# Cosformer attention with a multiplicative FFN: the query features of one batch transposed by DMA instead of TensorE, and the next loads issued later

## The chip, the cores and the metric

The kernel runs on one core of a Trainium2 chip. The metric is the device time of one execution in microseconds (us), as the median of several runs; lower is better. The profiled execution has a span (first to last recorded instruction) that is a little shorter than its device time.

## The reference

There are 8 batches of 8 heads, 576 positions and 64 dimensions per head, in float32. Attention is linear: the features of a row are its rectified values times a cosine and times a sine of its position, side by side, so 128 features per head.

```
q_p = phi(q, cos_w, sin_w)              # max(q, 0) * cos | max(q, 0) * sin
k_p = phi(k, cos_w, sin_w)
kv  = einsum('bhsf,bhsd->bhfd', k_p, v)
z   = sum(k_p, axis=2)
num = einsum('bhsf,bhfd->bhsd', q_p, kv)
den = einsum('bhsf,bhf->bhs', q_p, z)[..., None] + 1e-06
attn = num / den                        # then heads side by side: x, 4608 x 512
a = x @ w1;  b = x @ w2                 # 512 x 1024 each
out = (a * b @ w3) @ w_out              # 1024 x 1024, 1024 x 512
```

## The kernel before, in words

**The feed-forward part.** The 4608 tokens are taken in nine tiles of 512 (`t` from 0 to 8). The kernel forms `w3 @ w_out` once (`w34b`), so a tile needs `a` and `b` for eight column blocks (line 438), their product `abT` (a ScalarE copy on line 475, a VectorE product on line 479), and four blocks of 128 tokens times `w34b` (line 484), which ScalarE copies to `osb` (line 490) and a DMA that GpSimd issues stores (line 423).

**The attention part.** A batch has five chunks of rows, four of 128 and one of 64. Its steps are: `load` (lines 112 and 114: k, q and v of a batch, two DMAs each, issued by GpSimd, converted to bf16 on the way); `prep_k` and `prep_q` (features of a chunk: the cosine half on VectorE, line 251, the sine half on ScalarE, line 255); `prep_v` (a copy, from batch 2 on by GpSimd, line 275); `kv_chunk` (line 283: kv and z, summed over the five chunks, copied to `kvs` on lines 288 and 289); the transpose of each q chunk, 8 heads of 128 features, into `qpT`; `num` (line 341: `qpT` times `kvs`, then VectorE normalises to `xblk`, lines 349 to 351); and `x_tr`, which transposes `xblk` into its place in the 512-token tile `xT` of the feed-forward part. From batch 2 on `x_tr` is a DMA transpose that SyncE issues (line 373).

**Two ways to transpose a q chunk.** `q_tr` does it by eight TensorE transposes into a PSUM tile `pst` (line 314), which VectorE copies to `qpT` (line 316). The other way is a DMA transpose that SyncE issues at the end of `prep_q` (line 269). `dma_q(b)` names the chunks of batch `b` that take the second way: none of batches 0 to 2, two of batch 3, three each of batches 4 to 6, all five of batch 7.

**The order.** It is written out by hand: every engine runs its instructions in the order in which the program issues them. The generator `ffn_groups(t)` issues tile `t` in 24 groups: 16 for `a` and `b` (even groups a block of `a`, odd ones a block of `b`), then 8 for the output blocks. After group `g` the list `slots[g]` is issued. `attention_at` puts the steps of a batch into these slots (`kv`, `tr`, `nu`, `xt` give the slot of each chunk), and `spread` deals feature steps evenly over a stretch of slots. While tile 1 is computed (`t == 1`), batch 2 goes through attention (q features and v copies in slots 0 to 4, `kv` in slots 2 to 6, `q_tr` in slots 3, 5, 7, 9 and 11, `num` and `x_tr` in slots 8, 10, 12, 14 and 17), the features of batch 3 are made in slots 6 to 23, and batch 4 is loaded. A slot says where an instruction stands in its engine's order, not when it runs: GpSimd and SyncE take theirs as soon as the data and buffers that they need are there.

`ld` has two buffers for each of k, q and v, so the load of batch 4 writes the buffers of batch 2 and waits until its features are made. `num` has one PSUM buffer of two banks (`ps_att`), so a `num` waits for the normalisation of the one before it. Tile 2 of the feed-forward part begins with the first three chunks of batch 2 as its last 384 tokens.

Of the kernel before, what the change touches and what calls it, by code (L numbers as in the profile page):

```python
# [68 lines left out]
def kernel(  # L69
# [12 lines left out]
    B = q.shape[0]  # L82
# [64 lines left out]
    def feature_buffers(i):  # L147

        va = const.tile([P, NCH, H, D + 2], BF16, name=f"va{i}")
        nc.vector.memset(va[:, :, :, D:D + 1], 1.0)  # L150
        nc.vector.memset(va[64:128, 4, :, 0:D], 0.0)
        va_bufs.append(va)
        for name, bufs in (("kp", kp_bufs), ("qp", qp_bufs)):
            fp = const.tile([P, NCH, H, F], BF16, name=f"{name}{i}")
            nc.vector.memset(fp[64:128, 4, :, :], 0.0)
            bufs.append(fp)
# [46 lines left out]
    def w3_tr(jp):  # L203
        pst = ps_tr.tile([P, 8, 128], BF16, name="pst")
        for lc in range(8):
            nc.tensor.transpose(pst[:, lc, :], w3b[:, jp, ts(lc, 128)], identb[:])
        w3T = wst.tile([P, 8, 128], BF16, name="w3T")
        nc.vector.tensor_copy(out=w3T[:], in_=pst[:])
        w3Ts[jp] = w3T
# [14 lines left out]
    def order_of(b):  # L224

        return [0, 1, 2, 3, 4] if b % 2 == 0 else [4, 0, 1, 2, 3]

    def dma_q(b):

        return order_of(b)[5 if b < 3 else 3 if b == 3 else 2 if b < B - 1 else 0:]  # L230

    feat = {}

# [31 lines left out]
    def prep_q(b, c):  # L265
        features(b, feat_of(b)[1], raw[b, "q"], c)
        if c in dma_q(b):
            R = ROWS[c]
            nc.sync.dma_start_transpose(out=att_of(b)["qpT"][:, :, ds(columns_of(b, c), R)],
                                        in_=feat[b][1][:R, c].rearrange("p h f -> p (h f)"))  # L270
# [38 lines left out]
    def q_tr(b, c, evac=True):  # L309
        R = ROWS[c]  # L310
        qp = feat[b][1]
        pst = ps_tr.tile([P, 8, 128], BF16, name="pst")
        for h in range(H):
            nc.tensor.transpose(pst[:, h, :], qp[:, c, h, :], identb[:])  # L314
        dst, src = att_of(b)["qpT"][:, :, ds(columns_of(b, c), R)], pst[:, :, 0:R]
        on_vector = lambda: nc.vector.tensor_copy(out=dst, in_=src)  # L316
        on_scalar = lambda: nc.scalar.copy(out=dst, in_=src)
        if evac:
            on_vector()
        return on_vector, on_scalar  # L320
# [10 lines left out]
    def num(b, c, chain=True):  # L331
        rows = out_rows(b, c)
        R = ROWS[c]
        at = columns_of(b, c) - rows.start
        qpT, kvs = att[b]["qpT"], att[b]["kvs"]
        if b == 0 and c == 0:
            nt = ps_first.tile([P, 2, 512], FP32, name="pfirst")
        else:
            nt = ps_att.tile([P, 2, 512], FP32, name="pnum")
        for h in range(H):  # L340
            nc.tensor.matmul(nt[:, h // 4, ds((h % 4) * 65, 65)], lhsT=qpT[:, h, ds(at, 128)],  # L341
                             rhs=kvs[:, h, :], start=True, stop=True)
        n4 = nt[rows, :, 0:260].rearrange("p g (h e) -> p g h e", e=65)
        xblk = sm.tile([P, 2, 4, D], BF16, name="xblk", bufs=4)
        att[b]["x"][c] = xblk

        def normalize():
            den = sm.tile([P, 2, 4], FP32, name="den")
            nc.vector.tensor_scalar_add(out=den[rows], in0=n4[:, :, :, 64], scalar1=1e-6)
            nc.vector.reciprocal(out=den[rows], in_=den[rows])  # L350
            nc.vector.tensor_tensor(out=xblk[rows], in0=n4[:, :, :, 0:D],  # L351
                                    in1=den[rows].unsqueeze(3).to_broadcast([R, 2, 4, D]),
                                    op=ALU.mult)

        if chain:
            normalize()
        return normalize
# [3 lines left out]
    def x_tr(b, c, by_vector=False):  # L361
        R, rows = ROWS[c], out_rows(b, c)
        xblk = att[b]["x"].pop(c)
        xf = xblk[rows].rearrange("p g h d -> p (g h d)")
        if b % 2 == 0:
            slot = S * b + 128 * c
        else:
            slot = S * b + (0 if c == 4 else 64 + 128 * c)
        t, o = divmod(slot, 512)
        if t not in xT:  # L370
            xT[t] = xtp.tile([P, 4, 512], BF16, name="xT")
        if b >= 2:
            nc.sync.dma_start_transpose(out=xT[t][:, :, ds(o, R)], in_=xf)
            return
        pst = ps_tr.tile([P, 8, 128], BF16, name="pst")
        for kc in range(4):
            nc.tensor.transpose(pst[:, kc, 0:R], xf[:, ts(kc, 128)], identb[rows, rows])
        copy = nc.vector.tensor_copy if by_vector else nc.scalar.copy
        copy(out=xT[t][:, :, ds(o, R)], in_=pst[:, 0:4, 0:R])  # L379
# [131 lines left out]
    def spread(units, first, last, slots):  # L511
        for i, u in enumerate(units):
            slots[min(last, first + int(i * (last + 1 - first) / len(units)))].append(u)
# [32 lines left out]
    for t in range(NT):  # L546
        slots = [[] for _ in range(24)]
        if t == 0:
            slots[1].append(lambda: x_tr(0, 1, by_vector=True))
            slots[1].append(lambda: q_tr(0, 3, evac=False)[1]())  # L550
            slots[1].append(lambda: num(0, 2))
            slots[3].append(lambda: x_tr(0, 2))
            slots[3].append(lambda: num(0, 3))
            slots[4].append(lambda: x_tr(0, 3))
            slots[6].append(lambda: prep_q(0, 4))
            slots[11].append(lambda: feature_buffers(1))
            slots[8].append(lambda: q_tr(0, 4))
            slots[10].append(lambda: num(0, 4))
            slots[12].append(lambda: x_tr(0, 4))
            slots[14].append(lambda: w3_tr(0))  # L560
            between = [[] for _ in range(32)]
            later = [[] for _ in range(24)]
            spread(prep_units(1, (prep_k,)), 6, 8, between)
            spread(prep_units(1, (prep_q,)), 10, 12, between)
            spread(prep_units(1, (prep_v,)), 13, 13, between)
            attention_at(1, between, kv=(14, 14, 14, 14, 15), tr=(12, 13, 17, 18, 19),
                         nu=(16, 17, 18, 20, 22), xt=(18, 19, 20, 22, 25))
            later[:8] = between[24:32]
            for jp in range(8):
                for part in range(2):  # L570
                    if part == 0 and jp < 7:
                        slots[15].append(lambda jp=jp: w3_tr(jp + 1))
                    slots[15].append(lambda jp=jp, part=part: w34_mm(jp, part))
                    slots[15] += between[2 * jp + part]
            for g in range(16, 24):
                slots[g] += between[g]
            slots[16].append(lambda: load(3, "kqv"))
            spread(prep_units(2, (prep_k,)), 20, 23, slots)
        elif t == 1:
            for g in range(24):  # L580
                slots[g] += later[g]
            spread(prep_units(2, (prep_q,)), 0, 4, slots)
            spread(prep_units(2, (prep_v,)), 0, 4, slots)
            attention_at(2, slots, kv=(2, 3, 4, 5, 6), tr=(3, 5, 7, 9, 11),
                         nu=(8, 10, 12, 14, 17), xt=(8, 10, 12, 14, 17))
            for g, name in ((1, "k"), (8, "q"), (15, "v")):
                slots[g].append(lambda name=name: load(4, name))
            each = [u for c in zip(*(prep_units(3)[i:i + NCH] for i in (0, 5, 10))) for u in c]
            spread(each, 6, 23, slots)
        else:  # L590
            if t + 3 < B:
                for g, name in ((1, "k"), (8, "q"), (15, "v")):
                    slots[g].append(lambda name=name: load(t + 3, name))
            if t + 1 < B:
                attention_at(t + 1, slots, kv=(0, 1, 2, 3, 4), tr=(2, 4, 7, 10, 13),
                             nu=(6, 8, 11, 14, 17), xt=(6, 8, 11, 14, 17))
            if t + 2 < B:
                each = [u for c in zip(*(prep_units(t + 2)[i:i + NCH] for i in (0, 5, 10))) for u in c]
                spread(each, 0, 22, slots)
        for g, _ in enumerate(ffn_groups(t)):  # L600
            for u in slots[g]:
                u()
# [30 lines left out]
```

## Time and profile before

| what | value |
|---|---|
| median of 9 runs | 258.79 us (258.68 to 259.16) |
| the profiled execution | 258.73 us, span 257.0 us |
| granted TensorE clock, mean | 0.996 |
| TensorE matmul busy | 247.0 us, 96% of the span |
| VectorE, ScalarE, GpSimd busy | 145.9, 128.0, 86.0 us |
| bytes moved by DMA | 37.11 MB |

PE is TensorE's matmul work, PEld its weight loads (which run beside it), DVE is VectorE, ACT is ScalarE, POOL is GpSimd, SP is SyncE; POOLq and SPq are the instruction queues that issue DMAs. A row of a timeline gives start and length in us, the engine, the line, and output and inputs by name. In a table by stretch the columns are the stretch, its length, and the busy time of each engine with the number of its instructions, then the granted clock, the busy share of the DMA engines and their rate. The share of a DMA queue can exceed 100%, since one engine has several packets under way.

### The profile page before, as it was taken

Reading aid. Unit: us, or ns where it says so; the run is one execution under the profiler, and the core shown is the slowest. Engines: PE = TensorE matmul, PEld = TensorE weight load, DVE = VectorE, ACT = ScalarE, POOL = GpSimd, SP = SyncE. Lnnn points to the kernel's source line nnn. Section 1 sums busy time; section 2 is a strip of 40 time slices with the busy share of each in tenths; the row PEclk is TensorE's granted clock in tenths of the full one; section 3 lists DMA queues with packets and bytes.
Section 4 is the critical chain, followed back from the end, with each engine's and each line's share of the span. In section 5 each row is a group of like instructions: output and inputs, shape, how many; then the busy total and the mean of one; then the engine's idle time right before and its main releaser. Section 6 shows DMA issues by size and latency. Waiting matters only on the chain.

```text
span 257.0 us, 5053 instructions
## 1 busy us (share of the span) xinstructions
PE 247.0 (96%) x1934; PEld 135.0 (53%) x1967; DVE 145.9 (57%) x346; ACT 128.0 (50%) x219; POOL 86.0 (33%) x147
## 2 busy tenths in 40 slices
PE   8889999999999999999999999999999999999992
PEld 2478565655565465546554645555455544444441
DVE  6875755757879549824871787278526614303310
ACT  2775326727956555555655465646523233323321
POOL 7665244530760583048205900700230031022000
PEclk9999999999999999999999999999999999999998
DMA  7999999999999599999998999826490252024025
GB/s 194 183 193 202 209 204 202 199 199 198 245 164 137 99 203 188 161 165 162 188 154 182 178 195 133 180 46 134 93 193 13 57 125 66 0 43 123 1 44 122
DMA packets 68025, 37.11 MB, mean 144 GB/s; under 512 B 35616, under 2 KB 64544, under 8 KB 68000
## 3 DMA queue, kind: packets, MB, share of 16 engines
q0 software_dynamic: 35488, 27.20, 65.9%
q1 hardware_dynamic: 32352, 9.44, 21.0%
q8 instruction: 15, 0.25, 0.4%
q10 hardware_dynamic: 160, 0.13, 0.2%
q14 instruction: 10, 0.08, 0.1%
HBM read 38.80 MB, written 9.44 MB: 188 GB/s over the span
## 4 chain that ended last, share of the span: by engine, by line
PE 72%; DMA 20%; issue 2%; ACT 2%; POOL 1%; DVE 1%; ACTq 0%; POOLq 0%
PE ffnps L438 42%; PE ffnps L484 21%; DMA ks<-in_k_dram 10%; DMA qs<-in_q_dram 7%; DMA w2b<-in_moe_w_dram 3%; PE pnum L341 3%; PE pnum L283 3%; PE pst L314 2%; ACT kp L255 1%; POOL vs L120 0%; PE ffnps L501 0%; ACT osb L503 0%; POOL w2b L190 0%; POOL w1b L178 0%; DVE xblk L351 0%
## 5 line engine op out<-in xcount | busy, mean ns | idle before, releaser
L479 DVE TENSOR_TENSOR abT<-asb,ffnps 128x512 bf16<-128x512 bf16 x68 | 46.4, 683 | 64.1 <-PE ffnps L438 57.6
L438 PE MATMUL ffnps<-xT,w1b 128*128 128x512 bf16 (+2 forms) x312 | 74.4, 357 | 0.9 <-DVE xT L379 0.3
L438 PE MATMUL ffnps<-xT,w2b 128*128 128x512 bf16 (+2 forms) x306 | 73.2, 357 | 0.5
L475 ACT CAST asb<-ffnps 128x512 bf16<-128x512 f32 x68 | 39.8, 585 | 63.1 <-PE ffnps L438 55.7
L484 PE MATMUL ffnps<-w34b,abT 128*128 128x512 bf16 x273 | 63.3, 379 | 0.4
L423 POOL DMA_DIRECT2D out_dram<-osb x42 | 22.3, 536 | 119.7 <-ACT osb L490 119.6
L438 PEld LDWEIGHTS <-w1b 128*128 128x128 bf16 x320 | 28.8, 98 | 27.5 <-issue 0.8
L484 PEld LDWEIGHTS <-abT 128*128 128x128 bf16 x280 | 26.5, 98 | 30.3 <-DVE abT L479 0.4
L438 PEld LDWEIGHTS <-w2b 128*128 128x128 bf16 x320 | 27.4, 97 | 22.7
L490 ACT COPY osb<-ffnps 128x512 f32<-128x512 f32 x35 | 20.5, 585 | 37.9 <-PE ffnps L484 36.7
L255 ACT ACTIVATE qp<-qs,sinv 128x512 bf16<-128x512 bf16 (+2 forms) x40 | 28.2, 716 | 1.5 <-DMA qs<-in_q_dram 1.5
L351 DVE TENSOR_TENSOR xblk<-pnum,den 128x512 bf16<-128x512 f32 (+1 forms) x39 | 26.9, 691 | 1.4
L255 ACT ACTIVATE kp<-ks,sinv 128x512 bf16<-128x512 bf16 (+1 forms) x35 | 24.9, 721 | 0.0
L341 PEld LDWEIGHTS <-qpT 128*128 128x128 bf16 x320 | 15.1, 98 | 8.9 <-DVE xblk L351 0.9
L275 POOL COPY va<-vs 128x512 bf16<-128x512 bf16 (+1 forms) x30 | 18.4, 642 | 0.0
L251 DVE TENSOR_SCALAR qp<-qs,cosv 128x512 bf16<-128x512 bf16 (+1 forms) x40 | 18.0, 456 | 0.6 <-DMA qs<-in_q_dram 0.6
L341 PE MATMUL pnum<-kvs,qpT 128*128 128x65 bf16 x312 | 16.5, 194 | 0.3 <-DVE kvs L289 0.3
L283 PEld LDWEIGHTS <-kp 128*128 128x128 bf16 x280 | 12.7, 98 | 5.2
L316 DVE COPY qpT<-pst 128x1024 bf16<-128x1024 bf16 (+1 forms) x20 | 12.4, 618 | 5.0 <-PE pst L314 4.9
L218 PE MATMUL ffnps<-woutb,w3T 128*128 128x512 bf16 x61 | 15.0, 379 | 0.1
L314 PEld LDWEIGHTS <-qp 128*128 128x128 bf16 x184 | 12.0, 98 | 4.7
L283 PE MATMUL pnum<-va,kp 128*128 128x65 bf16 x280 | 14.1, 194 | 0.0
(81 smaller groups left out, 179.2 us busy)
## 6 DMA issues: line engine op xcount, KB each, us to landing
out_dram<-osb POOLq DMA_DIRECT2D x16, 256.0 KB, 3.9
out_dram<-osb POOLq DMA_DIRECT2D x24, 128.0 KB, 3.0
qs<-in_q_dram POOLq DMA_DIRECT2D x9, 256.0 KB, 7.7
ks<-in_k_dram POOLq DMA_DIRECT2D x7, 320.0 KB, 6.3
qs<-in_q_dram POOLq DMA_DIRECT2D x7, 320.0 KB, 7.0
vs<-in_v_dram POOLq DMA_DIRECT2D x7, 320.0 KB, 8.6
w3b<-in_moe_w_dram POOLq DMA_DIRECT2D x8, 256.0 KB, 13.1
ks<-in_k_dram POOLq DMA_DIRECT2D x7, 256.0 KB, 7.2
```

Of the source, the lines that this page charges most:

```text
L251: nc.vector.tensor_scalar(out=dst[:R, c, :, 0:D], in0=src[:R, :, c, :], scalar1=0.0, scalar2=cosv[:R, at:at + 1], op0=ALU.max, op1=ALU.mult)
L255: nc.scalar.activation(out=dst[:R, c, 0:n, D:F], in_=src[:R, 0:n, c, :], func=ACTF.Relu, scale=sinv[:R, at:at + 1], bias=0.0)
L275: eng.tensor_copy(out=feat_of(b)[2][:R, c, :, 0:D], in_=raw[b, "v"][:R, :, c, :])
L283: nc.tensor.matmul(kvt[:, h // 4, ds((h % 4) * 65, 65)], lhsT=kp[:, c, h, :], rhs=va[:, c, h, 0:D + 1], start=(i == 0 and h % 4 == 0), sto ...
L341: nc.tensor.matmul(nt[:, h // 4, ds((h % 4) * 65, 65)], lhsT=qpT[:, h, ds(at, 128)], rhs=kvs[:, h, :], start=True, stop=True)
L351: nc.vector.tensor_tensor(out=xblk[rows], in0=n4[:, :, :, 0:D], in1=den[rows].unsqueeze(3).to_broadcast([R, 2, 4, D]), op=ALU.mult)
L423: on.dma_start(out=rows[:, :, cols], in_=osb[64 * i:64 * i + rows.shape[0], :, cols])
L438: nc.tensor.matmul(out, lhsT=w[:, kc, ts(jc, 128)], rhs=x[:, kc, tok], start=(kc == 0), stop=(kc == 3))
L475: nc.scalar.copy(out=asb[:], in_=aT[:, :])
L479: nc.vector.tensor_mul(out=abT[:, jc, :], in0=asb[:], in1=bT[:, :])
L484: nc.tensor.matmul(ops[:, :], lhsT=abT[:, jc, ts(ms, 128)], rhs=w34b[:, jc, :], start=(jc == 0), stop=(jc == 7))
L490: nc.scalar.copy(out=osb[:, ms % 2, :], in_=ops[:, :])
```

## The change

For batch 2 all five chunks of q are now transposed by DMA: `prep_q` issues the transpose on SyncE behind the features of each chunk (slots 0 to 4 of `t == 1`), and `attention_at` no longer issues `q_tr` for them. The loads of batch 4 go from slots 1, 8 and 15 to slots 8, 13 and 18.

```
-        return order_of(b)[5 if b < 3 else 3 if b == 3 else 2 if b < B - 1 else 0:]
+        return order_of(b)[5 if b < 2 else 0 if b == 2 else 3 if b == 3 else 2 if b < B - 1 else 0:]
...
-            for g, name in ((1, "k"), (8, "q"), (15, "v")):
+            for g, name in ((8, "k"), (13, "q"), (18, "v")):
                 slots[g].append(lambda name=name: load(4, name))
```

## The prediction

> **What bounds the kernel now.** I read the page first. TensorE is busy for 96% of the span, but so are the DMA engines until two thirds of it, so the two rows by slices don't settle which of them counts while batch 2 is worked on.
>
> ```profile
> PE 247.0 (96%) x1934; PEld 135.0 (53%) x1967; DVE 145.9 (57%) x346; ACT 128.0 (50%) x219; POOL 86.0 (33%) x147
> ...
> PE   8889999999999999999999999999999999999992
> ...
> DMA  7999999999999599999998999826490252024025
> ```
>
> Then the chain that ended last: up to 61.2 us it runs through DMAs, from 64.1 us to 251 us through TensorE almost without a break (the piece at 192.8 us, 0.67 us on ScalarE, is the exception). The change acts from 66 us on. So the question is what TensorE does in tile 1. I cut the trace at the first product of tiles 1, 2, 3 and of tiles 6, 7 (timeline of TensorE), and asked for the table by stretch.
>
> ```profile
> 64.13:90.14 26.01, 25.80 (x216) 14.24 (x220) 19.91 (x48) 17.88 (x31) 12.60 (x21) 1.00 0.98 162
> 90.14:114.76 24.62, 24.41 (x197) 13.28 (x200) 16.27 (x37) 13.58 (x23) 10.22 (x17) 1.00 1.11 180
> 187.27:210.55 23.28, 23.07 (x173) 11.94 (x176) 10.74 (x24) 7.30 (x13) 3.15 (x7) 1.00 0.39 83
> ```
>
> The reader should see that matmul time fills each of the three tiles (25.80 of 26.01 us in the first) at a full granted clock, and that they differ in length. Tile 1 holds five q transposes on TensorE, tile 2 three, tile 6 none: 24.62 - 23.28 = 1.34 us for three is 0.447 us a chunk. The timeline of TensorE shows the same from start to start: eight transposes take 76.30 - 75.86 = 0.44 us. (The 0.61 us beside them is the length up to the modelled end of the last, not the time they hold the engine.)
>
> ```profile
> 75.86 0.61 PE L314 MATMUL pst<-identb,qp 128*128 128x128 bf16 x8
> 76.30 1.03 PE L438 MATMUL ffnps<-xT,w1b 128*128 128x512 bf16 x4
> 77.17 0.42 PE L341 MATMUL pnum<-kvs,qpT 128*128 128x65 bf16 x8
> ```
>
> **What is removed.** Five chunks, 40 transposes: 5 x 0.447 = 2.23 us of TensorE in a stage where nothing else ends last. Five copies on VectorE (line 316, 3.1 us in all) go too. VectorE is the nearest other engine there: 9.72 of the 10 us from 74 to 84 are busy. In that window it loses 0.60 + 0.60 + 0.34 = 1.5 us (start to start), TensorE two transposes, 0.9 us; so 8.2 us of VectorE stand in 9.1 us and it doesn't become the bound on the mean. I count nothing for its relief, though two `num` in the window waited for `xblk` (0.9 us of weight-load idle, 0.1 us of matmul idle).
>
> **What is added: five DMA transposes.** A chunk is 256 KB (the last 128 KB). Their issue costs SP about 1.25 us each; SP has nothing before 76.98 us, where the first `xT` transpose stands, so no one queues behind them. ScalarE ends the sine halves of the five chunks at 66.9, 68.0, 69.1, 69.7 and 71.0 us, VectorE its cosine halves no later than 0.2 us behind. With 1.25 us each on SP the issues fall at about 66.9, 68.2, 69.4, 70.7 and 71.9 us. How long they take beside loads is the disputed cost, and these are the nearest rows:
>
> ```profile
> DMA to landing us min/median/max: 2.7/3.7/6.1
> ...
> q1 hardware_dynamic: 1413, 0.35, 70.6%
> q0 software_dynamic: 732, 0.38, 69.1%
> ```
>
> The first is line 269 over the 16 chunks of the other batches; the two others are the queues from 103 to 107 us, where loads (q0) and transposes (q1) run together and each moves about 0.09 MB a us. With the longest landing, 6.1 us, they are there at 73.0, 74.3, 75.5, 76.8 and 78.0 us. They are due where `num` starts, which today is 74.73, 77.17, 79.60, 81.73 and 84.70 us, less 0.447 us for each transpose gone ahead of it (3, 4, 5, 5, 5): 73.4, 75.4, 77.4, 79.5 and 82.5 us. So all five are in time, the first by 0.4 us, the third by 1.9 us. Low bound of the cost: nothing. High bound: no row shows five in a row beside loads, and a half-size `xT` transpose issued at 124.58 us, with loads under way, took 7.3 us; that case is the slow rival below. I take nothing, because the rows are nearer: in time order from 68.6 us, at 1.25 us a chunk and 1.73 MB of loads at the 198 GB/s of the load-only stretch from 40 to 60 us, the queue would be c0, c1, half of k (1.6 us), c2, the rest of k (1.3 us), c3, half of q (1.6 us), c4, and c2 ends at 74.0, c3 at 76.5, c4 at 78.8 us.
>
> The page "VectorE: DVE Perf Modes" of the Trainium skill, section "Rules for kernel authors", speaks against the change: it advises TensorE for a 128x128 transpose if a PSUM destination will do, and its section "The three transpose paths" gives 390 ns there and 1309 ns by DMA. By those figures, taken serially, a chunk of eight would need 10.5 us by DMA, the third would land near 100 us and the change would lose some 20 us; the trace differs, since no chunk took over 6.1 us from issue to landing.
>
> **The `xT` transposes** of batch 2 stand behind them on SP and in the ring. The one that matters is the third, the last that tile 2 needs: its `xblk` is ready at 81.7 - 2.2 = 79.4 us, and even with 7.3 us it is there at 86.7 us, where tile 2 begins at 90.14 - 2.23 = 87.9 us. It goes at nothing, with 1.2 us in hand.
>
> **The loads of batch 4.** GpSimd's timeline shows what slots mean for them.
>
> ```profile
> 66.01 1.17 POOL L275 COPY va<-vs 128x512 bf16<-128x512 bf16 x2
> 67.13 0.70 POOL L112 DMA_DIRECT2D ks<-in_k_dram  x1
> 67.82 0.71 POOL L114 DMA_DIRECT2D ks<-in_k_dram  x1
> 68.50 1.81 POOL L275 COPY va<-vs 128x512 bf16<-128x512 bf16 x3
> 71.32 0.68 POOL L112 DMA_DIRECT2D qs<-in_q_dram  x1 [1.01 <-ACT qp L255]
> ...
> 73.77 0.70 POOL L112 DMA_DIRECT2D vs<-in_v_dram  x1
> ```
>
> GpSimd runs ahead of TensorE: v, in slot 15, is issued at 73.8 us, when TensorE is only about to begin group 8. In the new order k stands behind all five copies of batch 2, so it goes out at about 68.9 us, 1.7 us later. q then follows two copies of batch 3 and still waits for the last q features of batch 2 (71.0 us): 71.4 us, as today. v follows at about 73.5 us. All three stay ahead of the store that waits until 85.78 us (slot 18 is the last before it), which would have been the trap. The gain from moving them is nothing, except 1.7 us of DMA time left to the first two transposes. The copies that move ahead of k come 1.4 us earlier and were not waited for. The loads will land later since they share with the transposes, by up to the 1.18 MB of the chunks, 6 us at 198 GB/s: today they land by 81.5 us, then by 87.5 us at worst; batch 4's features begin with tile 2, k first, and k is there near 76 us. Cost nothing, 6 us of cover for k and q.
>
> **The sum.** 258.73 (profiled run; span 257.0 and 1.7 around it) - 2.23 = 256.50; the median of the runs lies 0.06 above that execution, so 256.5 to 256.6. From tile 2 on everything is the same work 2.2 us earlier: loads there are issued behind stores that TensorE paces. Forecast: 256.5, its own range 256.0 (the 0.2 us idle in tile 1 and VectorE's relief recovered, and 0.2 of error) to 257.0 (a chunk some tenths late).
>
> **Rivals.**
>
> *The transposes starve beside the loads (slower).* Place: third chunk, before `num` in slot 12. For: the `xT` transposes of 99.94 and 124.58 us took 6.7 and 7.3 us, and the queues from 99 to 103 us show load packets alone. If chunk 3 and on move only when the loads are through, near 80 us, it lands at 81.3 us, 3.9 us after it is due; the fourth, at 82.6, is then in time. 258.8 + 3.9 - 2.2 = 260.5. It decides when the third chunk lands after 79.6 us. Against: k alone doesn't fill the DMA engines (138 GB/s from 68.5 to 73.5 us), just when chunks 2 and 3 go.
>
> The page "DMA: Bandwidth & Descriptors", section "Issuing engines are not separate DMA queues", says that DMAs from all engines interleave on the same 16; sharing gives c3 near 76 us and no loss, starving the 260.5.
>
> *VectorE becomes the bound.* Its chain from `num` to `xblk` must fit 1.99 us in place of 2.43. If it doesn't speed up, the two transposes of 74 to 84 us bring nothing: 257.4. Against: the mean above.
>
> *Late by a little.* The first chunk has 0.4 us in hand, the third `xT` 1.2 us; a slip of 0.5 to 1.7 us in all gives 257.1 to 258.3.
>
> *No change.* The slip eats all 2.2 us (the third chunk near 79.6 us, or `xT` 2.2 us late for tile 2): 258.3 to 259.3.
>
> **Chances.** Forecast 0.68, VectorE 0.06, a little late 0.07, no change 0.06, slower 0.13. A difference of 0.2% (0.5 us) is about what a measurement of this kernel can tell from none. Faster by more: 0.68 + 0.06 + 0.06 = 0.80; within: 0.07; slower by more: 0.13. The range goes from 256.0 to 259.0, leaving out the slow rival and a little below.
>
> **What would show it.** Right: tile 1, from its first product to that of tile 2, takes 23.8 us; line 314 has 144 transposes; `num` of batch 2 starts near 73.4, 75.4, 77.4, 79.5 and 82.5 us, and its weight loads wait for no DMA; k of batch 4 is issued near 68.9 us, q and v where they were. Wrong: a wait of line 341 for `qpT` or of line 438 for `xT` in 73 to 90 us, chunks landing over 6.1 us after issue, or a chain that leaves TensorE after 64 us.

## The result, and the profile after

The changed kernel is slower: a median of 261.94 us (259.95 to 265.64, ten runs) against 259.07 us for the kernel before on the same chips, a ratio of 1.0109 with a 95% interval of 1.0095 to 1.0123. The forecast was 256.5 us, its range 256.0 to 259.0. The profiled execution took 265.64 us (span 263.9), longer than the other nine (up to 262.69); the ratios here and below leave out executions more than 1.5% above the fastest of their kernel, of which this is one, and the medians keep them. A second profile of the same kernel, from a later measurement, took 260.06 us (span 258.3). Both are used below.

The page of the changed kernel, the rows that answer to those of before, and one group of part 5:

```profile
PE 247.5 (94%) x1894; PEld 133.5 (51%) x1927; DVE 144.4 (55%) x341; ACT 127.8 (48%) x219; POOL 85.9 (33%) x147
...
PE   8889999999984799999999999999999999999993
...
PEclk9999999999998599999999999999999999999998
DMA  7999999999999969999999899953781234005015
...
L341 PE MATMUL pnum<-kvs,qpT 128*128 128x65 bf16 x312 | 16.7, 195 | 6.8 <-DMA qpT<-qp 5.6
```

TensorE has 40 matmuls fewer, but a hole in its 13th and 14th slices (about 79 to 92 us), with a fall of the granted clock, and `num` (line 341) now waits 5.6 us for `qpT` transposes. The table by stretch, from the first product of a tile to that of the next (tiles 1, 2 and 6):

```profile
64.56:97.48 32.92, 26.27 (x178) 12.60 (x180) 19.02 (x43) 17.67 (x31) 12.60 (x21) 0.90 1.12 162
97.48:122.10 24.62, 24.41 (x198) 13.28 (x201) 15.61 (x37) 13.59 (x23) 10.22 (x17) 1.00 1.11 179
194.60:217.88 23.28, 23.12 (x174) 11.93 (x176) 10.74 (x24) 7.31 (x13) 3.15 (x7) 1.00 0.39 83
```

Tiles 2 and 6 take exactly what they took before (24.62 and 23.28 us). All of the loss of this execution is in tile 1: 32.92 us in place of 26.01, where 23.8 was forecast. The `num` rows of batch 2 in TensorE's timeline say where:

```profile
73.82 0.42 PE L341 MATMUL pnum<-kvs,qpT 128*128 128x65 bf16 x8
...
76.85 0.43 PE L341 MATMUL pnum<-kvs,qpT 128*128 128x65 bf16 x8 [0.88 <-DVE kp L251]
...
82.90 0.43 PE L341 MATMUL pnum<-kvs,qpT 128*128 128x65 bf16 x8 [3.90 <-DMA qpT<-qp]
...
87.46 0.62 PE L341 MATMUL pnum<-kvs,qpT 128*128 128x65 bf16 x8 [1.72 <-DMA qpT<-qp]
...
92.04 0.42 PE L341 MATMUL pnum<-kvs,qpT 128*128 128x65 bf16 x8
```

The brackets give TensorE's idle time before each: 0.88 + 3.90 + 1.72 = 6.5 us. (The 0.88 us is put down to VectorE; the second chunk landed at 76.80 us, 0.05 us before this `num`, so I count it to the transposes.) The granted clock is 0.50 from 84.5 to 91.0 us, with 4.79 us of matmuls in it, which is an estimated 2.4 us lost. 23.8 + 6.5 + 2.4 = 32.7 us accounts for tile 1 of this execution. In the second profile the waits are shorter and the clock stays at 1.00; its tile 1 by stretch, and two `num` rows of its timeline:

```profile
64.53:91.85 27.32, 24.00 (x180) 11.93 (x180) 16.91 (x43) 17.67 (x31) 12.67 (x21) 1.00 1.23 195
```

```profile
78.82 0.43 PE L341 MATMUL pnum<-kvs,qpT 128*128 128x65 bf16 x8 [0.58 <-DMA qpT<-qp]
...
83.56 0.43 PE L341 MATMUL pnum<-kvs,qpT 128*128 128x65 bf16 x8 [2.58 <-DMA qpT<-qp]
```

So this execution pays 3.3 us of idle time (27.32 - 24.00) and nothing for the clock. The changed kernel ran 17 times in the two measurements. In ten of them the mean clock was 0.992 or less, where the kernel before has 0.995 to 1.000, and the time 261.65 to 265.64 us; in seven it was 0.997 or more and the time 259.95 to 261.91 us, still above the 258.6 to 259.4 us of the kernel before. So more than half of the executions seem to pay for the clock as well. But the profile with the lower clock also has the longer waits, so these times don't part the two.

The Trainium skill, page "TensorE: Matmul & The Clock Gate", section "Part 1: The HAM clock gate", says that the clock halves after an idle window of about 3.4 us. That agrees with 0.50 after the wait of 3.90 us in the one profile and 1.00 after 2.58 us in the other. A third trace does not fit: in the kernel with the transposes alone (below) the clock is 0.50 from 88 to 90 us after a wait of 2.40 us, so the length of one wait doesn't decide it here.

Issue to landing in this stage of the changed kernel (first profile), first of line 269 (`qpT`, five chunks), then of line 373 (`xT`, the four issued from 75 to 90 us):

```profile
DMA to landing us min/median/max: 3.7/11.8/13.0
```

```profile
DMA to landing us min/median/max: 3.3/6.1/8.5
```

The five chunks took 3.7, 7.0, 11.8, 13.0 and 12.6 us. SP needed 1.24 to 4.45 us to issue one.

### The profile page after: what moved, and what is told of

It reads as the page before. It is cut to its first block, busy times and chain, and to the rows that moved or that the text cites. A ratio compares the mean times of both kernels' runs of the same rounds, so it can differ in the third digit from the quotient of the medians.

```text
span 263.9 us, 4983 instructions
## 1 busy us (share of the span) xinstructions
PE 247.5 (94%) x1894; PEld 133.5 (51%) x1927; DVE 144.4 (55%) x341; ACT 127.8 (48%) x219; POOL 85.9 (33%) x147
## 4 chain that ended last, share of the span: by engine, by line
PE 80%; DMA 12%; ACT 2%; DVE 2%; issue 2%; POOL 1%; ACTq 0%; POOLq 0%
PE ffnps L438 44%; PE ffnps L484 20%; DMA qs<-in_q_dram 7%; DMA qpT<-qp 5%; PE ffnps L218 4%; PE pnum L341 3%; PE pnum L283 3%; PE pst L314 2%; PE pst L206 1%; ACT kp L255 1%; PE pst L377 1%; DVE va L275 0%; DVE qpT L316 0%; POOL vs L120 0%; ACT qpT L317 0%
## 5 line engine op out<-in xcount | busy, mean ns | idle before, releaser
L438 PE MATMUL ffnps<-xT,w2b 128*128 128x512 bf16 (+2 forms) x306 | 74.2, 360 | 0.6
L349 DVE TENSOR_SCALAR den<-pnum 128x8 f32<-128x8 f32 (+1 forms) x39 | 6.4, 163 | 18.0 <-PE pnum L341 17.4
L251 DVE TENSOR_SCALAR kp<-ks,cosv 128x512 bf16<-128x512 bf16 (+1 forms) x35 | 12.7, 376 | 0.1
## 6 DMA issues: line engine op xcount, KB each, us to landing
out_dram<-osb POOLq DMA_DIRECT2D x16, 256.0 KB, 4.0
qs<-in_q_dram POOLq DMA_DIRECT2D x9, 256.0 KB, 8.5
qs<-in_q_dram POOLq DMA_DIRECT2D x7, 320.0 KB, 10.6
w3b<-in_moe_w_dram POOLq DMA_DIRECT2D x8, 256.0 KB, 13.1
ks<-in_k_dram POOLq DMA_DIRECT2D x7, 256.0 KB, 8.1
```

What stands on the lines that cost most here:

```text
L251: nc.vector.tensor_scalar(out=dst[:R, c, :, 0:D], in0=src[:R, :, c, :], scalar1=0.0, scalar2=cosv[:R, at:at + 1], op0=ALU.max, op1=ALU.mult)
L438: nc.tensor.matmul(out, lhsT=w[:, kc, ts(jc, 128)], rhs=x[:, kc, tok], start=(kc == 0), stop=(kc == 3))
```

## The experiments

Theory A: the transposes are slowed by batch 4's loads beside them. Theory B: five in a row are slow by themselves. Times are medians; ratios are to the kernel before on the same chip, with 95% intervals.

### One half of the change at a time

Transposes only:

```
-        return order_of(b)[5 if b < 3 else 3 if b == 3 else 2 if b < B - 1 else 0:]
+        return order_of(b)[5 if b < 2 else 0 if b == 2 else 3 if b == 3 else 2 if b < B - 1 else 0:]
```

> Only the first half of the change: batch 2's q chunks by DMA, batch 4's loads left in slots 1, 8 and 15. Theory A (the transposes are slowed by the loads of batch 4 that run beside them): the k load goes out near 67.1 us, ahead of most transposes, so chunks 2 and 3 land no earlier than in the changed kernel; 261 to 264 us. Theory B (five chunk transposes in a row are slow by themselves on SP's queue, loads or not): about as the changed kernel, 262 us. If the later loads are what costs, this kernel is near 256.6.

Measured: 266.91 us, ratio 1.0311 (1.0287 to 1.0335), worse than both theories said. With the k load issued at 67.3 us, beside the first transpose, the chunks land 10.0, 13.0, 16.0, 11.3 and 7.8 us after issue; tile 1 takes 33.85 us. So the later loads did help in the change, by 5 us. The last of its waits is the one that the clock of 0.50 from 88 to 90 us follows (TensorE's timeline):

```profile
86.23 0.43 PE L341 MATMUL pnum<-kvs,qpT 128*128 128x65 bf16 x8 [2.40 <-DMA qpT<-qp]
```

Loads only:

```
-            for g, name in ((1, "k"), (8, "q"), (15, "v")):
+            for g, name in ((8, "k"), (13, "q"), (18, "v")):
```

> Only the second half: the loads of batch 4 in slots 8, 13 and 18, all q chunks of batch 2 still transposed by TensorE. A and B alike: k goes out 1.7 to 2 us later, q and v where they were, nobody waits for them; 258.8 to 259.2 us, no difference.

Measured: 258.92 us, ratio 0.9995 (0.9986 to 1.0004). By themselves they change nothing.

### The transposes without loads beside them

To the changed kernel, ahead of the loads in slot 8:

```
+            def gate():
+                seen2 = sm.tile([P, 1], BF16, name="seen2", bufs=1)
+                nc.gpsimd.tensor_copy(out=seen2[:], in_=att[2]["qpT"][:, 0, S - 1:S])
+            slots[8].append(gate)
```

> The changed kernel, but a GpSimd copy of one column of qpT (chunk 4 of batch 2) into a small tile stands ahead of batch 4's loads, so that no load of batch 4 is issued before the last chunk transpose of batch 2 has landed. A: each chunk lands within 5 us of its issue, no num waits for qpT, tile 1 takes 23.8 to 25 us; 256.6 us, up to 258 if the xT transposes, now beside the loads, come late for tile 2. B: chunks still take 7 to 13 us, 261 us or more, since the loads start later as well.

Measured: 264.14 us, ratio 1.02 (1.0167 to 1.0234); the time is a miss for A, yet tile 1 behaves as A said. The landing of the five chunks, then the `num` rows of batch 2 in TensorE's timeline, then tiles 1, 2 and 3 by stretch:

```profile
DMA to landing us min/median/max: 2.8/3.3/3.8
```

```profile
73.33 0.42 PE L341 MATMUL pnum<-kvs,qpT 128*128 128x65 bf16 x8
...
75.32 0.42 PE L341 MATMUL pnum<-kvs,qpT 128*128 128x65 bf16 x8
...
77.31 0.42 PE L341 MATMUL pnum<-kvs,qpT 128*128 128x65 bf16 x8
...
79.29 0.42 PE L341 MATMUL pnum<-kvs,qpT 128*128 128x65 bf16 x8
...
82.14 0.42 PE L341 MATMUL pnum<-kvs,qpT 128*128 128x65 bf16 x8
```

```profile
64.07:88.08 24.01, 23.67 (x181) 12.11 (x180) 17.32 (x43) 17.98 (x32) 12.62 (x22) 1.00 1.10 174
88.08:117.80 29.72, 24.78 (x201) 13.18 (x201) 15.34 (x37) 13.99 (x24) 12.90 (x22) 0.98 1.38 185
117.80:144.55 26.75, 26.75 (x193) 13.76 (x194) 14.90 (x36) 13.02 (x22) 7.52 (x13) 0.90 1.11 161
```

Alone, five chunks in a row land 3.3 us after issue (median): B falls. Tile 1 is 24.01 us. But the loads, now issued from 76.5 us on, take up to 13.6 us to land, the `xT` transposes and stores beside them up to 9.6 and 12.3 us, and the two q chunks of batch 3 that go by DMA 14.8 and 15.8 us. The bill comes a tile later: tile 3 starts after a wait of 4.94 us for `xT`, and at a lower clock, 0.90 in the mean (TensorE's timeline).

```profile
117.80 1.89 PE L438 MATMUL ffnps<-xT,w1b 128*128 128x512 bf16 x4 [4.94 <-DMA xT<-xblk]
```

### The transposes with nobody waiting for them

To the kernel before with the later loads, in `prep_q` (w3b is no longer read by then):

```
+        if b == 2:
+            R = ROWS[c]
+            nc.sync.dma_start_transpose(out=w3b[:, :, ds(columns_of(b, c), R)],
+                                        in_=feat[b][1][:R, c].rearrange("p h f -> p (h f)"))
```

> q chunks of batch 2 transposed by TensorE as before, loads in slots 8, 13, 18 as in the change, and besides the five DMA transposes are issued as in the change, but into columns of w3b that nobody reads any more: the transposes without anyone waiting for them. A and B: they still land 7 to 13 us after issue, since the loads (or their own number) do it and not TensorE's wait; the time is 259 us if the xT transposes behind them still come before tile 2, 260 to 261 if these come late. If they land within 6 us, the long landings of the changed kernel are a consequence of its stall and not the cause.

Measured: 264.01 us (260.80 to 266.45), ratio 1.015 (1.0079 to 1.0221), more than the 260 to 261 expected. The landing of the five unread transposes, then the first product of tile 2 in TensorE's timeline (line 438, shifted to 442 by the added lines):

```profile
DMA to landing us min/median/max: 4.0/11.2/14.6
```

```profile
93.91 1.86 PE L442 MATMUL ffnps<-xT,w1b 128*128 128x512 bf16 x4 [3.82 <-DMA xT<-xblk]
```

No `num` waited for these transposes, and the third to fifth landed as late as in the change (11.2, 14.6 and 12.5 us after issue). TensorE's stall is a consequence, not the cause. The `xT` transposes behind them landed 8.8 to 12.4 us after issue (four of the five) and held up tile 2.

### How many chunks, and which

In each, `dma_q(2)` returns the list named, and the loads stand in slots 8, 13 and 18 unless said otherwise:

```
+        if b == 2:
+            return [0, 3, 4]
```

The lists are [0], [0, 1], [3, 4], [2, 3, 4] and [0, 3, 4]; with "loads behind chunk 1" the copy shown above for the gated kernel stands in slot 8 too, and reads column 255 of `qpT`, the last of chunk 1.

> Of batch 2 only chunk 0 goes by DMA (the other four by TensorE), loads in slots 8, 13, 18. Theory A (transposes and loads slow each other where they overlap, TensorE's time per transpose is saved in full where they do not): chunk 0 is issued near 67 us, before the k load, lands in under 4 us, saves 0.45 us: 258.5 us against 259.0. Theory B2 (any chunk transpose in this stage costs more DMA time than the stage has): 259 us or more, with xT late for tile 2.

> Chunks 0 and 1 by DMA, three by TensorE, loads in slots 8, 13, 18. A: chunk 1 overlaps the k load and lands about 76 us, near the start of its num (75.8): between 258.2 (in time) and 259.2 us (late by up to 1 us).

> As the one with chunks 0 and 1 by DMA, but a GpSimd copy of the last column of chunk 1 stands ahead of batch 4's loads, so they begin when chunk 1 has landed, near 72.5 us, 3 us later than without. A: both chunks land in under 4 us, no num waits, 258.1 us, unless the loads, then ending near 83 us, hold up the xT transposes beyond the start of tile 2 (89.2 us): then 258.5 to 260.

> Chunks 3 and 4 by DMA (issued near 70 and 72 us, among the loads), 0 to 2 by TensorE, loads in slots 8, 13, 18: as many chunks as with 0 and 1, but all of it beside the loads. A: they land 7 to 13 us after issue, 78 to 83 us, the xT transposes behind them late as well; num 3 is due near 81.7, so 258.3 (just in time) to 260.5 us, and not better than chunks 0 and 1. B (number counts, not the overlap): the same time as with chunks 0 and 1.

Of the next five expectations, the first two were written for edits that the kernels which ran did not contain: the first was the changed kernel once more (the second profile above; 260.99 us, ratio 1.0078, 1.0047 to 1.0109), the second the kernel before once more (259.1 us, ratio 1.0001, 0.9993 to 1.001). Their expectations, then the runs that had the edits:

> Chunks 2, 3 and 4 by DMA, 0 and 1 by TensorE, loads in slots 8, 13, 18; against two chunks (257.6 us) one more chunk, 256 KB. If the stage has DMA time for it: 0.45 us less, 257.2. If two chunks have used up what there was (their third xT transpose landed 2 us before tile 2): chunk 2 lands in time, but 3 and 4 and the xT behind them are up to 3 us late, 258 to 261 us.

> Chunks 3 and 4 by DMA and batch 4's loads left in slots 1, 8 and 15: the better kernel without the second half of the change. If the later loads matter only where the DMA engines are overfull: 257.6 us, as with them. If the k load that goes out 1.7 us earlier holds up the transposes here as it does with five chunks (266.9 against 261.9 us): 258 to 260.

> Chunks 2, 3 and 4 by DMA, 0 and 1 by TensorE, loads in slots 8, 13, 18 (the last named run of this sort held the changed kernel itself; this one has the edit). One chunk of 256 KB more than with chunks 3 and 4 (257.6 us). If the DMA engines have time for it before tile 2: 257.2. If they share out what they have, so that everything beside the loads lands later together: chunk 2 in time, 3 and 4 about 11 us after issue, the third xT transpose near the start of tile 2: 257.5 to 259.5.

> Chunks 3 and 4 by DMA, loads of batch 4 in slots 1, 8 and 15 as before the change (the last run so named held the kernel before). With room on the DMA engines the place of the k load does not matter: 257.6 us, as with the later loads. If it matters here as with five chunks (266.9 against 261.9): 258 to 260.

> Chunks 0, 3 and 4 by DMA, 1 and 2 by TensorE, loads in slots 8, 13, 18. Three chunks again, but the first lands before the loads begin (3.7 us after issue in every kernel with the later loads). If only what overlaps the loads is slowed: 257.2 us, better than chunks 2, 3 and 4. If the number of chunks decides: the same as chunks 2, 3 and 4.

| chunks by DMA | of these beside the loads | tile 1, us | median, us | ratio (95%) |
|---|---|---|---|---|
| none (before) | 0 | 26.01 | 258.79 | |
| none, later loads | 0 | 25.77 | 258.92 | 0.9995 (0.9986 to 1.0004) |
| 0 | 0 | 25.29 | 258.24 | 0.997 (0.996 to 0.9979) |
| 0, 1 | 1 | 25.20 | 257.92 | 0.9958 (0.9946 to 0.9971) |
| 0, 1, loads behind chunk 1 | 0 | 25.58 | 257.79 | 0.9953 (0.9942 to 0.9965) |
| 3, 4 | 2 | 24.89 | 257.62 | 0.9946 (0.9933 to 0.996) |
| 3, 4, loads as before | 2 | 25.15 | 257.83 | 0.9954 (0.9942 to 0.9965) |
| 0, 3, 4 | 2 | 24.40 | 257.12 | 0.9928 (0.9917 to 0.994) |
| 2, 3, 4 | 3 | 25.81 | 258.61 | 0.9982 (0.9969 to 0.9994) |
| all five (the change) | 4 | 32.92 and 27.32 | 261.94 | 1.0109 (1.0095 to 1.0123) |

One chunk gains, so B2 falls. Of the two kernels with two chunks, A said that 3 and 4 would take 258.3 to 260.5 us; they took 257.62, no more than 0 and 1 (the intervals overlap). That is a miss for A: the two chunks landed 7.3 and 8.0 us after issue, at 77.31 and 79.49 us, and their `num` stood at 81.09 and 83.94. Landing late costs nothing until it meets a `num`, and two chunks don't tell A from the number of chunks; three do. Three chunks can be the best kernel here or gain almost nothing, depending on whether two or three of them run beside the loads. With 2, 3 and 4 the last two `num` wait again (TensorE's timeline; the two added lines shift line 341 to 343):

```profile
80.97 0.43 PE L343 MATMUL pnum<-kvs,qpT 128*128 128x65 bf16 x8 [0.45 <-DMA qpT<-qp]
...
84.61 0.43 PE L343 MATMUL pnum<-kvs,qpT 128*128 128x65 bf16 x8 [0.61 <-DMA qpT<-qp]
```

With 0, 3 and 4 none does, the time is the 257.2 us expected if only what overlaps the loads is slowed, and tile 1 is filled to 24.24 of 24.40 us (by stretch):

```profile
64.21:88.61 24.40, 24.24 (x193) 13.04 (x196) 17.53 (x45) 17.77 (x31) 12.62 (x21) 1.00 1.22 197
```

The step fits the rate of the transposes beside loads. The queues from 72 to 84 us in the second profile of the changed kernel (queue, packets, MB, share of the engines):

```profile
q0 software_dynamic: 2495, 1.42, 87.6%
q1 hardware_dynamic: 2488, 0.61, 41.8%
```

That is 0.61 / 12 = 0.051 MB a us for all transposes together, less than half of what the loads get (0.118). Count 2.0 us from issue to the first data (3.3 us for a chunk alone, less its 1.25) and 0.25 MB a chunk, 0.125 for the last. Chunks 3 and 4, first issued at 70.05 us, should then be through at 70.05 + 2.0 + 0.375 / 0.051 = 79.4 us: the last landed at 79.49. Chunks 2, 3 and 4, first issued at 69.20: 83.5 us, measured 84.56. The changed kernel, chunk 2 issued at 70.15 in the second profile: 84.4, measured 86.03. This is an estimate, worked out afterwards with one rate, which was read from the last of the three kernels; it puts all three within 1.7 us.

### Filling TensorE's wait

To the changed kernel, 16 unread matmuls of zeros in slot 11 and 8 in slot 13:

```
+            def filler(n):
+                unread = ps_tr.tile([P, 512], FP32, name="pst")
+                for _ in range(n):
+                    nc.tensor.matmul(unread[:, :], lhsT=zeros[:, 0:128], rhs=zeros[:], start=True,
+                                     stop=True)
+            slots[11].append(lambda: filler(16))
+            slots[13].append(lambda: filler(8))
```

> The changed kernel with matmuls of zeros that nobody reads issued on TensorE ahead of two of the nums that wait: 16 (3.5 us) before num of chunk 2 and 8 (1.7 us) before num of chunk 3. If a part of the loss is the granted clock that falls to 0.50 after TensorE's stall (6.8 us of it in the profile, about 2.4 us of work lost): the waits end when the transposes land, whatever fills them, the clock stays near 1.0, and the time falls from 262 to 259.5 to 261 us. If the clock has no part: the same 262 us, or more by what the filling does not hide.

Measured: 262.36 us, ratio 1.0125 (1.0107 to 1.0142), a miss. The profiled execution has a clock of 1.00 throughout the stage, and no `num` waits: chunk 2 landed at 79.24 us, the `num` behind the filling stood at 81.31. So 5.2 us of filling was more than the waits of that execution (tile 1: 28.99 us), and it took the place of what it was to save. It doesn't settle what the clock costs on average.

## Why the prediction was wrong

**What bounds tile 1, and 0.447 us a chunk: right.** With the loads held back, `num` started at 73.33, 75.32, 77.31, 79.29 and 82.14 us against 73.4, 75.4, 77.4, 79.5 and 82.5 forecast, and tile 1 was 24.01 us, 0.34 of it idle, against 23.8; so VectorE did not become the bound there. In the changed kernel tiles 2 to 7 took what they took before. One chunk alone brought 0.3%, 0.7 to 0.8 us; tile 1 fell by 0.72 us, but the kernel with only the loads moved shows 0.24 us of difference in tile 1 as well, so that the rest of 0.27 us is not shown to be VectorE's relief.

**"I take nothing, because the rows are nearer": the step that failed.** It summed the DMA work in order of issue at 198 GB/s and had the third to fifth chunk through at 74.0, 76.5 and 78.8 us. They landed at 82.86, 87.41 and 89.29, in the second profile at 78.78, 83.51 and 86.03. The engines don't serve one transfer after the other but share between loads and transposes, so that what is under way together ends late together (the loads of batch 4 took up to 14.2 us, 7.1 before). The transposes' share was 0.051 MB a us, where my sum used 198 GB/s for both; the two queues together moved 2.03 MB from 72 to 84 us of the second profile, 169 GB/s.

The row that was quoted with 0.09 MB a us for each was misread. In the four us from 103 to 107 the queues don't run together throughout: from 102 to 104 us the load queue moved 669 packets and the transposes 10, from 105 to 107 us it was 151 and 1147. The stretch with both, from 104 to 105 us in the kernel before (queue, packets, MB, share), shows 0.12 and 0.06:

```profile
q0 software_dynamic: 237, 0.12, 87.1%
q1 hardware_dynamic: 256, 0.06, 46.9%
```

Counted as in the experiments from the forecast issue of chunk 2 at 69.4 us, 0.06 puts the last three chunks at 75.6, 79.7 and 81.8 us, where they were due at 77.4, 79.5 and 82.5: the fourth is late and the fifth has 0.7 us left. With the measured 0.051 it is 76.3, 81.2 and 83.7. These are estimates. They would have told against a cost of nothing, but still fall short of the landings in the second profile by 2 us and more, in part since chunk 2 was itself issued at 70.15 us. The 6.1 us taken as the longest landing came from chunks that met one another two at a time at most; it didn't bound five beside six loads.

**"1.25 us each on SP": too small** where the transfers back up: 1.24 to 4.45 us. The last chunk was issued at 76.66 us, in the second profile at 74.14, where 71.9 was forecast.

**The `xT` transposes, 7.3 us at most: wrong.** 8.5 us in the changed kernel, 10.6 in the second profile, 12.4 with the unread transposes, where they alone held up tile 2.

**The loads: right in their issue, not in their landing.** k, q and v went out at 69.2, 72.6 and 74.5 us (forecast 68.9, 71.4 and 73.5), ahead of the store, and moving them alone did nothing. But the last of v landed at 89.42 us, in the second profile at 87.63, where 87.5 was put as the worst, and k at 78.07 and 78.41, where 76 was expected; tile 2 kept its 24.62 us even so. That their new place saves two transposes from contention was said and priced at nothing; with five chunks it was worth 5 us, with two it is not told apart from nothing (257.83 and 257.62).

**The slow rival was the case that came**, but its place holds for the first profile alone: there the third chunk, before `num` in slot 12, landed after 79.6 us. In the second profile it landed at 78.78, cost 0.58 us, and the fourth chunk, which the rival had in time, cost 2.58 us. So its price of 260.5, near the measured 261.9, is in part luck; what it missed is the fourth chunk and the clock. Its word, starving, was too strong: the transposes went on, with 0.61 of the 2.03 MB that the two queues moved from 72 to 84 us. The Trainium skill, page "DMA: Bandwidth & Descriptors", section "Issuing engines are not separate DMA queues", has the right mechanism (all interleave on the same 16 engines); the prediction read it as "no loss", without asking what share each of the two gets. The figure of 1309 ns a block from "VectorE: DVE Perf Modes" (section "The three transpose paths") would make an estimated 10.5 us of a chunk; alone, a chunk took 3.3 us here.

**The stage's spare DMA time was never added up.** The rows by slices showed the DMA engines at 9 of 10 up to 160 us. The prediction asked of each transfer by itself whether it would be in time, not whether all of them together were. The gated kernel shows that the same work, moved out of the way of the chunks, is paid for at tile 3.

Open: why the profiled execution was so much slower than the others, what the clock adds in the mean, and why the last chunks landed later still than one rate says.

## What to carry to other kernels

Work that is moved from the engine that bounds a stage to DMA saves its time in full only as long as the DMA engines have time left in that stage and the next: here two chunks beside the loads and one ahead of them were 0.7% faster, five were 1.1% slower. Cost a transfer beside others by the rate that its kind had in a stretch of the trace with both under way throughout (narrow the stretch until both queues have packets in all of it), and everything queued behind it by the same rate, not by the order of issue. Where a part of a change is in the clear and a part isn't, the part in the clear can be taken alone: chunks 0, 3 and 4 at 257.12 us beat both kernels.

## What the runs showed of the hardware

**Two queues got the engines nearly packet for packet.** From 72 to 84 us in the second profile of the changed kernel the loads had 2495 packets and the transposes 2488; in the kernel before, from 104 to 105 us, it was 237 and 256. The bytes are not alike, since a load packet carried 569 bytes in the mean (1.42 MB / 2495) and a transpose packet 245 (0.61 MB / 2488). So the transposes got 30% of the bytes. The counts are not alike in every stretch (2114 and 2627 from 72 to 84 us in the first profile), and no run here changes the size of the packets, so it is not shown that this sets the share.

**A busy share that rises while the bytes fall.** In some stretches where transposes met the loads, the total fell as well. In the gated kernel, with transposes alone, the DMA engines moved 194 GB/s from 72 to 74 us at a busy share of 1.03; in the changed kernel (first profile) they moved 107 GB/s from 78 to 80 us at a busy share of 1.74 (by stretch, in this order):

```profile
72.00:74.00 2.00, 2.00 (x17) 1.04 (x16) 1.55 (x5) 2.00 (x5) 0.00 (x0) 1.00 1.03 194
```

```profile
78.00:80.00 2.00, 1.01 (x5) 0.28 (x3) 1.30 (x3) 0.91 (x2) 0.00 (x0) 1.00 1.74 107
```

With the unread transposes it was 65 GB/s from 74 to 76 us at 1.74. The changed kernel is back at 188 GB/s from 84 to 86 us, the one with unread transposes at 181 from 76 to 78 us. It is not so wherever the two meet: in the second profile they moved 173 to 187 GB/s in every two us from 74 to 86 us, at 1.32 to 1.42, not far from the 198 GB/s of loads alone from 40 to 60 us in the kernel before, at 1.37. I had not expected that a busy share could rise while the bytes fall; no run here shows what in the engines does it.
